# Half of wq of four heads on partitions 0 to 63: a decode step of attention and mixer on one core

## The chip, the core and the metric

The kernel runs on one core of a Trainium2 chip. Its engines are PE (matrix products; PEld is its loading of weights), DVE, ACT, POOL and SP. SP computes nothing here: it issues nearly every load, in order, and an instruction on SP that waits holds back all that stand behind it. The loads are carried by 16 DMA engines. The metric is the device time of one execution in microseconds (us).

## The reference

Two layers run over x of shape (2, 1, 512), each an attention block over a given cache and a token mixer, with a residual around each:

```
x = x + A(layernorm(x));  x = x + B(layernorm(x));  x = x + A(layernorm(x));  x = x + B(layernorm(x))
A: q = x @ wq (32 heads of 128);  p = softmax(q k^T / sqrt(128)) over 32768 keys;  (p v) @ wo
   8 key-value heads, 4 query heads on each; k and v are (2, 8, 32768, 128) in float32
B: u = gelu(layernorm(x)^T w1 + b1) with 1792 hidden units, then u w2 + b2, per channel
```

Both layers use the same weights and the same cache. All is float32.

## The kernel before

**Units.** A unit is (layer, batch, head): 2 x 2 x 8 = 32 of them. Each reads K and V of its batch and head once (16.8 MB each). A unit's K is 64 groups of 128 x 512, its V too; a step is four groups. `Order` lists all steps: the K steps of one unit, then the V steps of the unit before it, and so on. Only around the two places where a batch goes from layer 0 to layer 1 ("the changes") is the order another one, and some of K and V stays in SBUF and is used twice.

**Memory and loads.** The tile `mem` holds 106 cells of 128 partitions x 512 elements. A full load of K or V takes 32 cells (8.39 MB), so three of them and ten more cells fit. `plan_loads` decides while the program is built, from assumed times, which cells each load takes, how large it is and after which step it is issued; on the chip SP waits for semaphores until the cells are free. Around the changes the loads are small, and cells 90 to 105 go round among loads of four cells.

**Weights.** `wqo` holds for each head 4 cells of wq and 4 cells of wo. In nearly all of the program wq goes to cells 0 to 3, wo to cells 4 to 7. wq of a head is asked for 16 steps ahead of its first K step; wo of a head is in use until the `out_2` (L490) of its last unit.

**Queries.** `make_q` runs in three steps on PE and DVE. `wide_products` (L321) makes four products of a 128 x 32 column tile of `xw` (the normalized x, as columns) with 128 x 512 of wq, one for each quarter d of the 512 inputs, into four bands of 32 partitions of one PSUM tile; `narrow_products` (L328) adds the bands. The work sits among the V steps of the unit before, ten to six steps ahead of the K steps that need it.

**The rest.** K steps (L356) make scores, V steps (L424) make the weighted sums in `acc`, DVE and ACT do the softmax in between, `out_1` and `out_2` (L463, L490) multiply by wo. The last unit loads V in ever smaller pieces (16, 8, 4, 2, 1, 1 cells), and its mixer ends the program.

Of the kernel before, what the change touches and what calls it, by code (L numbers as in the profile page):

```python
# [8 lines left out]
F32 = mybir.dt.float32  # L9
# [4 lines left out]
P = 128  # L14
G = 512
# [5 lines left out]
WCELLS = 4  # L21
# [17 lines left out]
STEP_US = 1.6  # L39
ASK_Q = 16  # L40
ASK_O = 8


class Order:
# [75 lines left out]
def plan_loads(order, weights, busy):  # L120

    steps = order.steps
    step_of = {(kind, u, g + i): p for p, (kind, u, g) in enumerate(steps) for i in range(STEP)}
    from_kept = set(order.kept.values()) | set(order.held.values())
    asked = [(p, kind, u, g + i) for p, (kind, u, g) in enumerate(steps) for i in range(STEP)]
    asked = [a for a in asked if a[1:] not in from_kept]  # L130
    weights = sorted(weights)
    last_use = [-1] * CELLS
    landed, done, loads = {}, [], []
    queue, array, begun, i = 2.0, 0.0, -1, 0

    def ready(cells):
        t = 0.0
        for c in cells:
            if last_use[c] >= len(done):
                return None  # L140
            if last_use[c] >= 0:
                t = max(t, done[last_use[c]])
        return t

    while i < len(asked) or weights:
        if weights and (i == len(asked) or weights[0][0] <= asked[i][0]):
            _, name, last = weights.pop(0)
            label, sizes, stays = ("W", name, 0), (WCELLS,), True
        else:
            _, kind, u, g = asked[i]  # L150
            label, stays = (kind, u, g), (kind, u, g) in order.kept
            n = 1
            while (
                i + n < len(asked)
                and asked[i + n][1:] == (kind, u, g + n)
                and (g + n) % HALF
                and ((kind, u, g + n) in order.kept) == stays
            ):
                n += 1
            sizes = [s for s in SIZES if s <= n] or [n]  # L160
            if label in order.sizes:
                sizes = [min(order.sizes[label], n)]
        best = None
        for s in sizes:
            spots = range(CELLS - s + 1)
            found = None
            for a in spots if stays else reversed(spots):
                t = ready(range(a, a + s))
                if t is not None:
                    wait = max(0.0, t + LEAD_US - queue)  # L170
                    key = (wait, t if s == max(SIZES) or label[:2] == ("V", order.last) else 0.0)
                    if found is None or key < found[3]:
                        found = (wait, s, a, key)
            if found is not None and (best is None or found[0] < best[0] - 0.01):
                best = found
            if best is not None and best[0] == 0.0:
                break
        wait, s, a, _ = best
        begun = max(begun, *(last_use[a : a + s]))
        loads.append((label, s, a, begun))  # L180
        queue += wait + s * CELL_US + LOAD_US
        if label[0] == "W":
            last_use[a : a + s] = [last] * s
        else:
            for j in range(s):
                key = (kind, u, g + j)
                for k in (key, order.kept.get(key)):
                    if k is not None:
                        landed[k] = queue + LAND_US
                        last_use[a + j] = step_of[order.back.get(k, k)]  # L190
                if key in order.held:
                    landed[order.held[key]] = queue + LAND_US
            i += s
        while len(done) < len(steps):
            kind, u, g = steps[len(done)]
            keys = [(kind, u, g + j) for j in range(STEP)]
            if any(k not in landed for k in keys):
                break
            array = max(array, *(landed[k] for k in keys)) + STEP_US
            array += busy.get(len(done), 0.0)  # L200
            done.append(array)
    return loads


@with_exitstack
def gqa_mixer_kernel(ctx: ExitStack, tc: tile.TileContext, x, kt, v, wqo, cols, out):
    nc = tc.nc
    B, D = out.shape
    HKV = wqo.shape[0]
    R = wqo.shape[2] // (2 * D)  # L210
    DH = kt.shape[2]
    DT = D // P
# [7 lines left out]
    const = ctx.enter_context(tc.tile_pool(name="const", bufs=1))  # L220
# [10 lines left out]
    def cells(a, n):  # L231
        return mem[:, a * G : (a + n) * G]
# [18 lines left out]
    misc = pfix.tile([P, G], F32, name="misc")  # L251
    S = [const.tile([P, G], F32, name=f"S{k}") for k in range(2)]
    xw = const.tile([P, DT, 32], F32, name="xw")
    RAW = B
    xT = {}
    turn = [0, 0, 0]
# [7 lines left out]
    def constants():  # L264
# [4 lines left out]
        nc.gpsimd.memset(xw, 0.0)  # L269
        nc.gpsimd.memset(xw[:, :, RAW + 1], 1.0)  # L270
        nc.vector.tensor_reduce(
# [6 lines left out]
    def first_input():  # L278
# [16 lines left out]
        for b in range(B):  # L295
            xT[b] = xcols[:, b, :]
            nc.vector.tensor_scalar_mul(xw[:, :, b], cen[:, b, :], rs[:, b : b + 1])

    def row_tile():
        return work.tile([P, D], F32, name="row", bufs=1)  # L300

    wq_sb, wo_sb = {}, {}
    q_at, q_ps, q_row = {}, {}, {}
# [13 lines left out]
    def wide_products(us, wq):  # L317

        q_ps[us] = pfix.tile([P, G], F32, name="bcast")
        for d in range(DT):  # L320
            nc.tensor.matmul(q_ps[us][32 * d : 32 * d + 32, :], xw[:, d, :], wq[:, d, :], start=True, stop=True)  # L321

    def narrow_products(us, side):

# [289 lines left out]
    def change_0(key):  # L614
        xT[key[1]] = const.tile([P, DT], F32, name=f"xT_{key[1]}")
        nc.vector.tensor_add(xw[:, :, RAW], columns(key), sq)

# [141 lines left out]
    def at(p, f, *args, us=0.0):  # L759
        hooks.setdefault(p, []).append((f, args))  # L760
        busy[p] = busy.get(p, 0.0) + us
# [10 lines left out]
    for u in order.units:  # L772
        layer, b, h = u
# [5 lines left out]
        us = (u, mate) if b == 0 and mate not in made and (layer == 0 or h < HKV - 2) else (u,)  # L779
# [5 lines left out]
    for name, us in users.items():  # L785
        k0 = min(first["K", u] for u in us)
        h = name if isinstance(name, int) else name[1]
        layer = min(u[0] for u in us)
        v0 = min(first["V", u] for u in us)
        both = h >= HKV - 2  # L790
        weights.append((k0 - ASK_Q if k0 else -1, ("q", layer, h), max(first["K", u] for u in us) if both else k0))
        weights.append((k0 if both else v0 + ASK_O, ("o", layer, h), max(end["V", u, 1] for u in us) + 3))

    for u in order.units:
        layer, b, h = u
# [35 lines left out]
        e = v_end  # L831
# [23 lines left out]
        at(e + 3, unread, u, G)  # L855
        at(e + 4, change_3, y, us=1.0)
        at(e + 4, unread, u, G // 2)
        assert e + 4 < first["K", y]

    for x, _, y in order.changes:  # L860
# [10 lines left out]
    def load(label, n, a):  # L871
        kind, u, g = label
        if kind == "W":
            part, layer, h = u
            w = D * R
            at_w = 0 if part == "q" else w
            nc.sync.dma_start(cells(a, n), wqo[h][:, at_w : at_w + w])
            (wq_sb if part == "q" else wo_sb)[layer, h] = cells(a, n).rearrange("p (t c) -> p t c", t=DT)
            return
        layer, b, h = u  # L880
        src = (kt if kind == "K" else v)[b * HKV + h, g // HALF, :, (g % HALF) * G : (g % HALF + n) * G]
        nc.sync.dma_start(cells(a, n), src)
        for j in range(n):
            at_cell[kind, u, g + j] = a + j
            if (kind, u, g + j) in order.kept:
                at_cell[order.kept[kind, u, g + j]] = a + j
# [6 lines left out]
        load(label, n, a)  # L893
    constants()
    first_input()
    for step in range(3):
        make_q(opening_q, step)
    for p, (kind, u, g) in enumerate(steps):
# [8 lines left out]
def _layout(A_x, A_k_cache, A_v_cache, A_wq, A_wo, B_w1, B_b1, B_w2, B_b2):  # L907
    import numpy as np

    B, HKV, SK, DH = A_k_cache.shape  # L910
    D = A_x.shape[-1]
    U = B * HKV
    kt = A_k_cache.reshape(U, 2, NG, 32, 2, 2, 8, 2, 2, DH).transpose(0, 1, 9, 4, 7, 8, 2, 5, 6, 3)
    wq = A_wq.reshape(D // P, P, HKV, -1).transpose(2, 1, 0, 3)
    wo = A_wo.reshape(HKV, -1, DH, D).transpose(0, 2, 1, 3)
    w1, b1, w2 = (a.reshape(P, -1) for a in (B_w1, B_b1, B_w2))
    none = np.zeros_like(w2)
    w2z = np.stack([none, w2], axis=2).reshape(P, -1)
    cols = [w1, b1, w2z, none[:, :1], np.broadcast_to(B_b2.reshape(1, 1), (P, 1))]
    return {  # L920
        "x": np.ascontiguousarray(A_x.reshape(B * (D // P), P).T),
        "kt": np.ascontiguousarray(kt).reshape(U, 2, DH, HALF * G),
        "v": A_v_cache.reshape(U, 2, P, HALF * G),
        "wqo": np.concatenate([wq.reshape(HKV, P, -1), wo.reshape(HKV, DH, -1)], axis=2),
        "cols": np.concatenate(cols, axis=1),
    }


_INS = ["x", "kt", "v", "wqo", "cols"]


# [20 lines left out]
```

## Time and profile before

| | |
|---|---|
| median of 3 runs | 2503.35 us (2501.34 to 2504.8) |
| the profiled execution | 2500.76 us; its span, first to last instruction, 2498.1 us |
| busy | PE 56%, PEld 17%, DVE 8%, ACT 7% of the span |
| mean rate of the loads | 426 GB/s over the span, 1064.66 MB |
| matmul instructions of K steps, V steps | 4096, 4080 |

The page of the profile gives busy times by engine, the span in 40 slices, the DMA queues, the chain of work that ended last, and groups of instructions. The table by windows gives, for stretches of time, each engine's busy time, then the granted clock of TensorE, then the mean share of the 16 DMA engines that were busy, then the rate in GB/s. In short windows a transfer is counted where it falls, so a share can go a little above 1. A logical float32 product shows as two instructions on PE. In the timeline each row is a start, a duration, an engine, a line, what is written from what, a count, and in brackets how long the engine stood idle before it and for what.

### The profile page before, as it was taken

How to read it: one execution, taken by the hardware profiler on the slowest of the kernel's cores; microseconds unless marked ns; L12 is line 12 of the kernel's file. 1: busy time of each engine (PE TensorE's matmuls, PEld its weight loads, DVE VectorE, ACT ScalarE, POOL GpSimd, SP SyncE). 2: the span in 40 equal slices, each digit the busy share in tenths (PEclk: the TensorE clock that was granted, in tenths of full speed). 3: DMA queues.
4: the chain of work that ended last, by engine and by line, in shares of the span. 5: the costliest groups of instructions: out<-in, count | busy, mean ns of one | idle time of the engine just before them, and what ended most of it. 6: DMA issues, size and time to landing. Idle time of an engine off the chain costs nothing.

```text
span 2498.1 us, 21381 instructions
## 1 busy us (share of the span) xinstructions
PE 1393.4 (56%) x9754; PEld 412.7 (17%) x9754; DVE 188.6 (8%) x502; ACT 186.9 (7%) x581; POOL 5.1 (0%) x18
## 2 busy tenths in 40 slices
PE   3455455555555545556776775555555545564557
PEld 1111111111111111112121221111111111111113
DVE  1000000000000000001111010000000000000012
ACT  0100000000000000001110210000000000000021
POOL 0000000000000000000000000000000000000000
PEclk8777777777777777778887986777777777776788
DMA  9999999999999999999999999999999999999996
GB/s 420 435 435 431 431 435 429 435 426 434 436 431 435 433 425 436 425 435 406 417 430 423 418 427 437 431 434 434 428 434 431 436 432 429 435 435 433 432 428 272
DMA packets 34947, 1064.66 MB, mean 426 GB/s; under 512 B 4133, under 2 KB 4137, under 8 KB 5034
## 3 DMA queue, kind: packets, MB, share of 16 engines
q1 hardware_dynamic: 34568, 1063.27, 99.1%
q8 instruction: 76, 1.25, 0.2%
q14 instruction: 13, 0.11, 0.0%
q10 hardware_dynamic: 290, 0.04, 0.0%
HBM read 1063.29 MB, written 0.00 MB: 426 GB/s over the span
## 4 chain that ended last, share of the span: by engine, by line
DMA 64%; PE 25%; another core or an unknown queue 9%; issue 0%; DVE 0%; ACT 0%; SPq 0%; POOLq 0%; DVEq 0%
DMA mem<-in_v_dram 35%; DMA mem<-in_kt_dram 29%; PE acc L424 13%; PE scores L356 8%; PE misc L463 1%; PE rows L490 0%; PE misc L328 0%; PE bcast L321 0%; PE misc L447 0%; PE misc L380 0%; PE rows L724 0%; ACT S L406 0%; PE misc L374 0%; PE bcast L516 0%
## 5 line engine op out<-in xcount | busy, mean ns | idle before, releaser
L424 PE MATMUL acc<-mem,S 128*16 128x512 f32 x4080 | 594.7, 717 | 585.3 <-DMA mem<-in_v_dram 580.5
L356 PE MATMUL scores<-mem,qz 128*32 128x512 f32 x4096 | 613.6, 741 | 487.4 <-DMA mem<-in_kt_dram 487.2
L406 ACT ACTIVATE S<-S,neg 128x128 f32<-128x128 f32 x256 | 129.6, 509 | 2215.9 <-DVE S L401 1202.8
L356 PEld LDWEIGHTS scores<-mem,qz 128*32 128x32 f32 x4096 | 145.3, 129 | 887.9 <-issue 795.5
L424 PEld LDWEIGHTS acc<-mem,S 128*16 128x16 f32 x4080 | 127.5, 107 | 900.6 <-issue 808.6
L366 DVE TENSOR_REDUCE mx<-scores 128x1 f32<-128x512 f32 x64 | 44.3, 692 | 775.0 <-PE scores L356 767.2
L463 PEld LDWEIGHTS misc<-selg,row 128*128 128x128 f32 x256 | 48.9, 285 | 48.2 <-issue 36.8
L401 DVE STREAM_TRANSPOSE S<-scores 128x512 f32<-128x512 f32 x64 | 45.5, 710 | 126.4 <-PE acc L424 126.4
L463 PE MATMUL misc<-selg,row 128*128 128x4 f32 x256 | 51.7, 325 | 3.3 <-DVE row L455 3.3
L490 PE MATMUL rows<-mem,oz 128*2 128x512 f32 x248 | 51.2, 914 | 0.3 <-DVE oz L479 0.3
L406 ACT ACTIVATION_READ_ACCUMULATOR S<-S,neg 128x1 f32 x256 | 47.7, 187 | 0.0
L376 DVE TENSOR_REDUCE m<-misc 1x4 f32<-1x128 f32 x32 | 8.9, 279 | 379.5 <-PE misc L374 379.5
L455 DVE COPY row<-acc 128x512 f32<-128x512 f32 x32 | 22.1, 692 | 177.9 <-PE acc L424 177.9
L449 DVE RECIPROCAL rl<-misc 128x4 f32<-128x4 f32 x32 | 5.8, 183 | 352.8 <-PE misc L447 352.8
L479 DVE TENSOR_TENSOR oz<-misc,rl 128x4 f32<-128x4 f32 x32 | 5.2, 163 | 276.6 <-PE misc L463 276.2
L447 PEld LDWEIGHTS misc<-both,one 128*128 128x128 f32 x64 | 12.8, 250 | 51.5 <-issue 44.4
L321 PE MATMUL bcast<-mem,xw 128*32 128x512 f32 x144 | 20.0, 618 | 1.7 <-POOL x_rs L294 1.7
L328 PEld LDWEIGHTS misc<-selg,row 128*128 128x128 f32 x128 | 17.1, 208 | 18.7 <-issue 7.7
L328 PE MATMUL misc<-selg,row 128*128 128x2 f32 (+1 forms) x128 | 18.5, 266 | 0.8 <-DVE row L313 0.8
L574 ACT ACTIVATE row<-bcast,bias,scale 128x512 f32<-128x512 f32 x21 | 16.3, 778 | 31.6 <-PE rows L558 15.4
L447 PE MATMUL misc<-both,one 128*128 128x4 f32 x64 | 15.6, 315 | 5.2 <-DVE both L446 5.2
L374 PE MATMUL misc<-ident,mxa 128*1 128x128 f32 x64 | 17.1, 363 | 2.0 <-DVE mxa L372 2.0
(125 smaller groups left out, 263.4 us busy)
## 6 DMA issues: line engine op xcount, KB each, us to landing
mem<-in_v_dram SPq DMA_DIRECT2D x13, 4096.0 KB, 25.1
mem<-in_v_dram SPq DMA_DIRECT2D x37, 1024.0 KB, 9.0
mem<-in_kt_dram SPq DMA_DIRECT2D x15, 2048.0 KB, 17.6
mem<-in_kt_dram SPq DMA_DIRECT2D x30, 1024.0 KB, 9.1
mem<-in_wqo_dram SPq DMA_DIRECT2D x28, 1024.0 KB, 36.3
mem<-in_kt_dram SPq DMA_DIRECT2D x6, 4096.0 KB, 28.6
mem<-in_kt_dram SPq DMA_DIRECT2D x2, 6144.0 KB, 23.5
mem<-in_v_dram SPq DMA_DIRECT2D x3, 2048.0 KB, 38.2
```

Source lines behind the costliest of these rows:

```text
L321: nc.tensor.matmul(q_ps[us][32 * d : 32 * d + 32, :], xw[:, d, :], wq[:, d, :], start=True, stop=True)
L328: nc.tensor.matmul(pt[:, r * n : (r + 1) * n], q_row[us][:, r * DH : (r + 1) * DH], side, start=True, stop=True,)
L356: nc.tensor.matmul(sc_ps[u, half][32 * row : 32 * row + 32, :], qz[:, at : at + 32], cells(at_cell["K", u, g], 1), start=(i == 0), stop=(i ...
L366: nc.vector.tensor_reduce(mx[u][:, half : half + 1], sc_ps[u, half], axis=AX.X, op=ALU.max)
L374: nc.tensor.matmul(pm[:1, :P], mxa, ident, start=True, stop=True)
L401: nc.vector.transpose(S[half], sc_ps[u, half])
L406: nc.scalar.activation(s[:, :, h], s[:, :, h], AF.Exp, bias=neg[u][:, h : h + 1], scale=SCALE, accum_out=lsum[u][:, half, h : h + 1],)
L424: nc.tensor.matmul(acc[32 * row : 32 * row + R * QT, :], S[half][:, col : col + R * QT], vc, start=(g < NG), stop=(g >= quads - NG),)
L447: nc.tensor.matmul(pl[:, :R], ones, both, start=True, stop=True)
L455: nc.vector.tensor_copy(asb[u], acc)
L463: nc.tensor.matmul(po_of[u][:, :R], asb[u][:, t * DH : (t + 1) * DH], selg[:, t * R : (t + 1) * R], start=(t == 0), stop=(t == QT - 1 and ...
L490: nc.tensor.matmul(rows[32 * r : 32 * r + B, :], oT[u][:, 2 * r + 1 - b : 2 * r + 3 - b], wo_of(u)[:, r, :], start=False, stop=(u == order ...
```

## The change

For four heads (layer 0: 2 and 4; layer 1: 3 and 1) wq takes 6 cells instead of 4. The first two quarters of wq (d = 0, 1) are loaded as before, 128 partitions with half as long a row. The other two quarters (d = 2, 3) lie on partitions 0 to 63 alone, over four cells: of each quarter rows 0 to 63 in one cell and rows 64 to 127 in the next. They come from a new input `low`, by two transfers of 32 partitions each. In `low` every four rows are followed by a fifth that isn't read, so that the source has eight groups of four rows. The bytes that are read are the same, 1 MiB for each head.

The products of d = 2 and d = 3 become two each, over 64 rows: one with rows 0 to 63 of `xw`, one with `high`, a copy of rows 64 to 127 of `xw` on partitions 0 to 63. DVE makes `high` three times (`lift`): once at the start and once in each change. The scratch that is set aside for descriptors of POOL's queue becomes 256 instead of 512.

```diff
+LOWER = (("q", 0, 2), ("q", 0, 4), ("q", 1, 3), ("q", 1, 1))
+LOWER_CELLS = 6
...
-            label, sizes, stays = ("W", name, 0), (WCELLS,), True
+            label, sizes, stays = ("W", name, 0), (LOWER_CELLS if name in LOWER else WCELLS,), True
...
+    high = const.tile([P // 2, DT // 2, 32], F32, name="high")
...
+    def lift():
+
+        nc.vector.tensor_copy(high, xw[P // 2 :, DT // 2 :, :])
...
         for d in range(DT):
-            nc.tensor.matmul(q_ps[us][32 * d : 32 * d + 32, :], xw[:, d, :], wq[:, d, :], start=True, stop=True)
+            to = q_ps[us][32 * d : 32 * d + 32, :]
+            if d < DT // 2 or wq.shape[1] == DT:
+                nc.tensor.matmul(to, xw[:, d, :], wq[:, d, :], start=True, stop=True)
+                continue
+            half, k = P // 2, d - DT // 2
+            nc.tensor.matmul(to, xw[:half, d, :], wq[:half, DT // 2 + 2 * k, :], start=True, stop=False)
+            nc.tensor.matmul(to, high[:, k, :], wq[:half, DT // 2 + 2 * k + 1, :], start=False, stop=True)
...
+            if u in LOWER:
+                nc.sync.dma_start(cells(a, DT // 2), wqo[h][:, : w // 2])
+                for k in range(2):
+                    to = cells(a + DT // 2, DT)[32 * k : 32 * k + 32, :]
+                    nc.sync.dma_start(to, low[h, k][:, :4, :])
+                wq_sb[layer, h] = cells(a, n).rearrange("p (t c) -> p t c", t=n)
+                return
...
+    low = np.zeros((HKV, 2, 8, 5, 4 * G), np.float32)
+    part = wq[:, :, D // P // 2:, :].reshape(HKV, 2, 2, 8, 4, -1, G).transpose(0, 2, 3, 4, 5, 1, 6)
+    low[:, :, :, :4, :] = part.reshape(HKV, 2, 8, 4, 4 * G)
...
-    nc = bacc.Bacc("TRN2", target_bir_lowering=False, num_devices=1, dynamic_dma_scratch_size=512)
+    nc = bacc.Bacc("TRN2", target_bir_lowering=False, num_devices=1, dynamic_dma_scratch_size=256)
```

All K and V loads keep their sizes, their cells and their places in the order. For the four heads wq stands in cells 0 to 5 and wo in cells 6 to 9.

On SP, where the weights of head 2 are loaded in layer 0 (the first of the four places; `in_wqo_dram` holds the weights, PE_49 is a semaphore that PE raises), before:

```order
L882 DMA mem<-in_kt_dram 128x16384 [waits DMAHW5_49,PE_49]
L877 DMA mem<-in_wqo_dram 128x2048 [waits DMAHW1_49]
L882 DMA mem<-in_v_dram 128x16384 [waits DMAHW6_49,PE_49]
L877 DMA mem<-in_wqo_dram 128x2048 [waits PE_49]
L882 DMA mem<-in_v_dram 128x16384 [waits DMAHW7_49,PE_49]
```

The same place after:

```order
L903 DMA mem<-in_kt_dram 128x16384 [waits DMAHW5_49,PE_49]
L892 DMA mem<-in_wqo_dram 128x1024 [waits DMAHW1_49]
L895 DMA mem<-in_low_dram 32x1x2048 [waits PE_49]
L895 DMA mem<-in_low_dram 32x1x2048
L903 DMA mem<-in_v_dram 128x16384 [waits DMAHW6_49]
L898 DMA mem<-in_wqo_dram 128x2048 [waits PE_49]
L903 DMA mem<-in_v_dram 128x16384 [waits DMAHW7_49,PE_49]
```

The wait for PE that stood ahead of the load of wo (until L490 has read the wo of the head before, cells 4 and 5 of it) now stands ahead of the first `low` load as well, and so ahead of a V load that it did not hold before.

On PE, where the queries of head 2 in layer 0 are made, before:

```order
L424 MATMUL acc<-mem,S_89 16x512 x12
L321 MATMUL bcast<-mem,xw 32x512 x4
L424 MATMUL acc<-mem,S_89 16x512 x4
L424 MATMUL acc<-mem,S_90 16x512 x8
L447 MATMUL misc<-both,one 128x4
```

After:

```order
L437 MATMUL acc<-mem,S_89 16x512 x12
L330 MATMUL bcast<-mem,xw 32x512 x2
L333 MATMUL bcast<-mem,xw 32x512
L334 MATMUL bcast<-mem,high 32x512
L333 MATMUL bcast<-mem,xw 32x512
L334 MATMUL bcast<-mem,high 32x512
L437 MATMUL acc<-mem,S_89 16x512 x4
L437 MATMUL acc<-mem,S_90 16x512 x8
L460 MATMUL misc<-both,one 128x4
```

Two more products stand there, among the V steps of the unit before; nothing else moved.

More of the change, by code (lines that the diff above doesn't have):

```diff
@@ L205, in gqa_mixer_kernel @@
 @with_exitstack
-def gqa_mixer_kernel(ctx: ExitStack, tc: tile.TileContext, x, kt, v, wqo, cols, out):
+def gqa_mixer_kernel(ctx: ExitStack, tc: tile.TileContext, x, kt, v, wqo, low, cols, out):
     nc = tc.nc
@@ L857, in gqa_mixer_kernel @@
         at(e + 4, unread, u, G // 2)
+        at(e + 7, lift)
         assert e + 4 < first["K", y]
@@ L895, in gqa_mixer_kernel @@
     first_input()
+    lift()
     for step in range(3):
@@ L924, in _layout @@
         "wqo": np.concatenate([wq.reshape(HKV, P, -1), wo.reshape(HKV, DH, -1)], axis=2),
+        "low": low,
         "cols": np.concatenate(cols, axis=1),
     }
-_INS = ["x", "kt", "v", "wqo", "cols"]
+_INS = ["x", "kt", "v", "wqo", "low", "cols"]
 def kernel(A_x, A_k_cache, A_v_cache, A_wq, A_wo, B_x, B_w1, B_b1, B_w2, B_b2):
```

## The prediction

> **What bounds the kernel now.** I read the page first: busy times, DMA queues, the chain.
>
> ```profile
> span 2498.1 us, 21381 instructions
> ...
> PE 1393.4 (56%) x9754; PEld 412.7 (17%) x9754; DVE 188.6 (8%) x502; ACT 186.9 (7%) x581; POOL 5.1 (0%) x18
> ...
> q1 hardware_dynamic: 34568, 1063.27, 99.1%
> q8 instruction: 76, 1.25, 0.2%
> ...
> DMA 64%; PE 25%; another core or an unknown queue 9%; issue 0%; DVE 0%; ACT 0%; SPq 0%; POOLq 0%; DVEq 0%
> ```
>
> The loads' queue (q1) takes 99.1% of what 16 DMA engines have in the span. The engines are full, PE is not. Since the bytes stay the same, time can only come from engines that are full while others are not. So I looked for moments when the share falls, in the table by windows (the last two columns are DMA share and GB/s). First the steady state:
>
> ```profile
> 256.00:580.00 324.00, 168.77 (x1144) 48.87 (x1144) 19.26 (x50) 16.88 (x64) 0.00 (x0) 0.73 1.00 433
> ```
>
> Then the end of the last loads:
>
> ```profile
> 2471.00:2472.00 1.00, 1.00 (x12) 0.26 (x8) 0.00 (x0) 0.00 (x0) 0.00 (x0) 1.00 0.97 395
> 2472.00:2473.00 1.00, 1.00 (x16) 0.36 (x12) 0.00 (x0) 0.00 (x0) 0.00 (x0) 1.00 0.87 348
> 2473.00:2474.00 1.00, 1.00 (x15) 0.30 (x7) 0.00 (x0) 0.00 (x0) 0.00 (x0) 1.00 0.59 244
> 2474.00:2475.00 1.00, 0.36 (x4) 0.06 (x1) 0.00 (x0) 0.00 (x0) 0.00 (x0) 1.00 0.53 221
> 2475.00:2476.00 1.00, 0.88 (x10) 0.26 (x14) 0.00 (x0) 0.00 (x0) 0.00 (x0) 1.00 0.47 197
> 2476.00:2477.00 1.00, 1.00 (x14) 0.32 (x7) 0.00 (x0) 0.00 (x0) 0.00 (x0) 1.00 0.49 199
> 2477.00:2478.00 1.00, 1.00 (x27) 0.83 (x25) 0.69 (x1) 0.00 (x0) 0.00 (x0) 1.00 0.54 203
> 2478.00:2479.00 1.00, 1.00 (x28) 0.73 (x20) 0.00 (x0) 0.00 (x0) 0.00 (x0) 1.00 0.35 133
> 2479.00:2480.00 1.00, 1.00 (x20) 0.98 (x22) 0.00 (x0) 0.00 (x0) 0.00 (x0) 1.00 0.04 14
> ```
>
> The share doesn't fall to nothing. It falls to one half and stays there from 2473.5 to 2478.5: eight engines are done, eight have 5 us of work left. Every load is shared over all 16, so it has landed only when the late eight are done. Where the 5 us come from, the page's q8 row says: 76 fetches of instructions take 0.2% of 16 x 2498.1 us, that is 80 us (60 to 100 with the rounding). Spread over 16 engines this would be 5 us each and no difference. On eight of them it is 10 us each, about 5 in each half of the run.
>
> The same in the middle, at the first change:
>
> ```profile
> 1160.00:1175.00 15.00, 11.44 (x74) 3.27 (x74) 1.03 (x4) 2.11 (x8) 0.00 (x0) 0.77 0.99 415
> 1175.00:1180.00 5.00, 4.67 (x34) 1.83 (x34) 2.42 (x5) 2.66 (x9) 0.00 (x0) 1.00 0.82 313
> 1180.00:1185.00 5.00, 3.52 (x32) 1.98 (x35) 1.79 (x7) 2.05 (x4) 0.54 (x1) 1.00 1.05 382
> 1185.00:1190.00 5.00, 4.20 (x43) 1.33 (x39) 0.00 (x0) 3.27 (x5) 0.00 (x0) 1.00 0.98 392
> 1190.00:1195.00 5.00, 3.02 (x36) 0.83 (x32) 0.00 (x0) 2.89 (x4) 0.00 (x0) 1.00 1.00 388
> 1195.00:1205.00 10.00, 6.14 (x63) 2.41 (x56) 1.77 (x5) 4.38 (x6) 0.00 (x0) 1.00 1.02 425
> ```
>
> Between 1175 and 1195 some 1125 GB/s x us are missing against 425, which is 2.65 us of all engines or 5.3 us of eight. Here the loads go round among a few cells, so the early eight must wait for cells that PE frees only after the late eight have delivered. There they lose their lead, and in the second half of the run it grows again. So the late eight set the pace in both halves.
>
> **The change part by part.** *Bytes off the late eight.* At 433 GB/s one engine moves 27.06 GB/s. A wq load of 1 MiB is 64 KiB or 2.42 us on each. After the change the first half costs every engine 32 KiB, 1.21 us, and the `low` transfers, with eight groups of source rows, can fall on eight engines alone: 64 KiB or 2.42 us on each of these. So at each of four places eight engines save 1.21 us and eight pay 1.21 us more. Two places lie in each half of the run, so a lead of about 5 us shrinks by 4.84 to nearly nothing. If the late eight are the ones relieved, they finish 2.42 us earlier at the first change and 2.42 us earlier again at the end: -4.84 us. The paying eight stay at or ahead of them by then, so they cost nothing.
>
> Which eight? No row names the engine of a packet. But one other transfer leaves engines out:
>
> ```profile
> out_dram<-row ACTq DMA_DIRECT2D x1, 2.0 KB
> ```
>
> It is one row, so one engine carries it, and the records of single packets around it show that this engine ended its shares with the early eight. If a transfer of fewer groups starts from the same engine, `low` falls on the early eight. [...]
>
> *Less starving at the first change.* The 2.65 us missing there exceed the 2.42 that a lead of 4.84 on eight engines explains, and against the 433 of the steady state they would be more, some 3.2. What is left, 0 to 0.8 us, all engines lose while loads arrive apart. I take 0.4.
>
> *Shorter rows.* The first half has rows of 4 KB instead of 8, and there are eight more loads. No window holds such loads alone. From the long rows of the steady state (433 GB/s) to the 8 KB rows of the small loads (425, from 1195 to 1205) it is 2%; as much again for 4 KB is 0.02 us a place. I take +0.1 for all, between 0 and 0.3.
>
> *The wait on SP.* The order shows that the first `low` load waits for L490, and the V load behind it waits too.
>
> ```profile
> 197.93 0.42 SPq L877 DMA_DIRECT2D mem<-in_wqo_dram  x1
> 215.57 0.33 SPq L882 DMA_DIRECT2D mem<-in_v_dram  x1
> 231.13 1.93 PE L490 MATMUL rows<-mem,oz 128*2 128x512 f32 x8
> 233.12 0.33 SPq L877 DMA_DIRECT2D mem<-in_wqo_dram  x1
> 238.61 0.33 SPq L882 DMA_DIRECT2D mem<-in_v_dram  x1
> 266.95 3.62 PE L424 MATMUL acc<-mem,S 128*16 128x512 f32 x16 [12.03 <-DMA mem<-in_v_dram]
> 275.65 1.04 PE L321 MATMUL bcast<-mem,xw 128*32 128x512 f32 x8
> ```
>
> The V load goes out at about 233.5 instead of 215.57, 18 us later. PE got its data at 266.9. Its 8.39 MB take 19.4 us at 433 GB/s, so its first bytes moved at about 247.5. Issued at 233.5 it is still 14 us early, and so are the `low` loads ahead of it, which land near 250 and are read at 275.65. wo and the next V load (238.61) keep their times. Cost nothing, at the price of 18 of 32 us of cover.
>
> *Products and copies.* Two more logical products at four places are 16 instructions. The page's row for L321 prices them:
>
> ```profile
> L321 PE MATMUL bcast<-mem,xw 128*32 128x512 f32 x144 | 20.0, 618 | 1.7 <-POOL x_rs L294 1.7
> ```
>
> By 139 ns of busy time each (20.0/144) that is 0.6 us a place, by their own 618 ns 2.5 us. At 266.95 PE had idled 12.03 us for data, so either is hidden. A `lift` copies 64 x 64; DVE rows of the start price it:
>
> ```profile
> 9.97 0.36 DVE L297 TENSOR_SCALAR xw<-cen,x_rs 128x4 f32<-128x4 f32 x2 [0.83 <-POOL x_rs L294]
> 12.43 0.69 DVE L313 COPY row<-bcast 128x512 f32<-128x512 f32 x1 [2.10 <-PE bcast L321]
> 15.08 0.23 DVE L342 COPY qz<-misc 128x4 f32<-128x4 f32 x2 [1.96 <-PE misc L328]
> 25.83 8.52 PE L356 MATMUL scores<-mem,qz 128*32 128x512 f32 x64 [10.79 <-DMA mem<-in_kt_dram]
> ```
>
> It lies between 0.12 and 0.69 us, and the start has 10 us until data come. In the changes it stands between copying `acc` and the product by wo, where loads are late, not DVE.
>
> Sum: -4.84 - 0.4 + 0.1 = -5.1 us. The profiled execution (2500.76 us, 2498.1 of it span) would take 2495.7; the median of the runs shown, 2503.35, is 2.6 above it, so I forecast 2498.2. What a measurement here can tell from no change is about 0.2%, 5.0 us, which puts the border at 2498.3, almost on the forecast.
>
> **Rivals.** *The wrong eight.* If `low` falls on the late eight, these pay 4.84 us and the early ones wait longer: +4.84 and up to 0.8 more starving, 2508.2 to 2509.0. Against it stands the one-row transfer; for it, that no row names an engine.
>
> *Half-width transfers hold the others up* (the one on the slower side that I take most seriously). If all engines wait until `low` is done, each place costs 1.21 us more for everyone: +4.84, 2508.2, and with a gap of a microsecond behind each of eight transfers 2516. It decides as soon as the idle eight can't take up the next load. Against it: in the windows from 2473.5 to 2478.5 one half works on alone at half the rate, having been left behind by engines that went ahead through many loads. [...]
>
> *The queue runs dry.* If the wait for L490 ended 14 us later, the V load would be late at four places, a microsecond for each beyond that.
>
> *Half of it.* If what is won at the first change is lost there again (PE's chain, not the late eight, sets when cells come free), only the end's 2.42 stays: 2500.9.
>
> *The change doesn't do what it says.* If `low` is spread over all engines after all, nothing is moved: 2503.4.
>
> **How the numbers follow.** Forecast 0.76 (2496 to 2500, the border inside it, two thirds of it below since what starves at the change may give more); wrong eight 0.05; holding up 0.04; dry queue 0.02; half 0.08; no shift 0.05. Faster by over 0.2%: 0.52. Within: 0.24 of the forecast, half and no shift, 0.37. Slower: 0.11. The range 2496.0 to 2503.5 leaves out the slower cases and a little at the fast end.
>
> **What would show it.** In the changed profile the half share at the end should last 1 us or less instead of 5, and the rate from 1175 to 1195 should be near 420. SP should issue the V load at the four places near its wo load. The share in the steady windows should stay at 1.00 around 245 to 250. A half share at the end of 10 us would mean the wrong eight; a dip near 250 the holding up or the dry queue.

## The result, and the profile after

The changed kernel takes 2506.02 us (median of 15 runs, 2503.91 to 2510.49), the kernel before, measured together with it, 2500.57 us (15 runs, 2498.95 to 2504.8). The ratio is 1.0021 [1.0013, 1.0029]: 5.45 us slower, where 5.1 us faster was forecast. Two places show where it goes: the end of the last loads and the first change. First the page of the changed kernel:

```profile
span 2504.7 us, 21425 instructions
...
q1 hardware_dynamic: 34888, 1063.27, 98.9%
q8 instruction: 77, 1.26, 0.2%
```

The same bytes, the same full queue, one more fetch of instructions. Next the windows at the end of the loads and at the first change (columns as before: busy time by engine, clock, DMA share, GB/s):

```profile
2479.00:2480.00 1.00, 1.00 (x16) 0.24 (x12) 0.00 (x0) 0.00 (x0) 0.00 (x0) 1.00 0.88 358
2480.00:2481.00 1.00, 1.00 (x14) 0.30 (x7) 0.00 (x0) 0.00 (x0) 0.00 (x0) 1.00 0.85 332
2481.00:2482.00 1.00, 0.45 (x8) 0.13 (x2) 0.00 (x0) 0.00 (x0) 0.00 (x0) 1.00 0.49 193
2482.00:2483.00 1.00, 0.81 (x8) 0.25 (x12) 0.00 (x0) 0.00 (x0) 0.00 (x0) 1.00 0.33 117
2483.00:2484.00 1.00, 1.00 (x13) 0.28 (x6) 0.00 (x0) 0.00 (x0) 0.00 (x0) 1.00 0.16 66
2484.00:2485.00 1.00, 1.00 (x26) 0.82 (x22) 0.69 (x1) 0.00 (x0) 0.00 (x0) 1.00 0.13 53
2485.00:2486.00 1.00, 1.00 (x31) 0.72 (x20) 0.00 (x0) 0.00 (x0) 0.00 (x0) 1.00 0.13 49
2486.00:2487.00 1.00, 1.00 (x20) 0.98 (x23) 0.00 (x0) 0.00 (x0) 0.00 (x0) 1.00 0.07 29
```

```profile
1160.00:1175.00 15.00, 10.82 (x82) 3.09 (x74) 0.95 (x3) 2.11 (x8) 0.00 (x0) 0.88 1.00 421
1175.00:1180.00 5.00, 3.82 (x36) 1.44 (x32) 1.48 (x3) 0.57 (x3) 0.00 (x0) 1.00 0.90 374
1180.00:1185.00 5.00, 3.51 (x26) 0.81 (x22) 2.92 (x8) 3.09 (x9) 0.55 (x1) 1.00 0.88 333
1185.00:1190.00 5.00, 4.41 (x48) 2.34 (x40) 0.22 (x1) 2.19 (x4) 0.00 (x0) 1.00 0.93 339
1190.00:1195.00 5.00, 3.40 (x40) 0.90 (x34) 0.00 (x0) 3.60 (x6) 0.00 (x0) 1.00 0.95 329
1195.00:1205.00 10.00, 5.37 (x64) 1.36 (x54) 0.85 (x2) 5.83 (x9) 0.00 (x0) 1.00 0.99 392
```

The half share is gone, and in its place is a staircase. To 2481 some 14 engines work, and from 2483 to 2486 the share is 0.13 to 0.16: **two engines of 16** are still at it. At the first change 1625 GB/s x us are missing against 425 between 1175 and 1195 (20 x 425 less 5 x (374 + 333 + 339 + 329)) where 1125 were missing before. One profile doesn't settle that, though: the kernel called "The wait without the placement" below, whose median is that of the kernel before, misses 1540 in these windows of its own profile (342, 375, 336 and 339 GB/s).

The trace also holds the times at which a load's semaphore was raised, once by each engine that has delivered its share ("landings" below). A full load has 16 of them; a `low` transfer has eight, behind one record at its issue, so eight engines carry it. The landings don't name the engine, but they come in an order that hardly changes from one full load to the next: across each of the first 25 fetches of instructions in the profile before, 15 of the 16 landings keep their distances within 0.1 us, and one moves. So one engine can be followed. Here is one K load of the first half, shortly before the first change, in ns after its first landing:

```
before, at 881.75 us: 0 146 310 587 922 1382 1400 1458 | 4593 4613 4623 4687 4753 4805 4987 5473
after,  at 879.58 us: 0 51 | 4345 4421 4431 4512 4532 4618 4810 5006 5140 5969 5979 5997 | 9841 10294
```

Before: eight early, eight late, as the prediction read it. After: 2, 12 and 2. A place (one of the four loads of wq in the new way) puts 1.21 us more on each engine that carries `low` and takes 1.21 us from each other one (an estimate: 32 KiB at 27.06 GB/s, a sixteenth of the 433 of the steady state), so the two kinds move 2.42 us apart, and two places lie ahead of this load: 4.84 us. If two of the late eight are among the engines that carry `low`, then two early ones stay early, six early ones rise by 4.84 to where the late ones were, six late ones stay, and two late ones rise from about 5 to between 9.8 and 10.3, all counted from the first landing. These are the groups that the list shows.

That two of the eight are late ones can be seen without this sum, in the landings of `low` itself. Here is the first `low` transfer of each of the first two places, again in ns after its first landing:

```
first place,  at 245.19 us: 0 290 357 398 527 579 1251 2468
second place, at 566.03 us: 0 259 327 495 530 1219 1921 3935
```

Six of the eight keep their distances within 50 ns. Two don't: 398 becomes 1921, and 2468 becomes 3935, each 1.5 us later. Between the two places instructions were fetched at 299.6 and at 333.0 us, the eighth and the ninth fetch, and in the full loads behind each of the two one of these engines falls back.

What the two cost is seen in the last landing of a load. Of the K load above it comes 2.64 us later than before; in all nine full loads from 744 to 882 us it is 2.62 to 2.68. At the end of the last load the groups are the same:

```
before, at 2473.03 us: 0 96 136 239 665 888 1064 1176 | 5162 5931 6128 6142 6216 6311 6411 7045
after,  at 2476.04 us: 0 748 | 4734 4750 4865 5750 5795 6260 6380 6426 6568 7594 7642 7755 | 11022 11070
```

There the last landing comes 7.04 us later. Not all of that is from the places: between 1062 and 1261 us of the kernel before, over the first change, the delay of the last landing grew from 2.63 to 4.49 us, and in the kernel called "The wait without the placement" it grew as much (from 0.17 to 2.08).

The wait on SP and the added products are where they were expected: `low` goes out when `out_2` (now L503) ends at 233.20, and V right behind it (timelines of SP, then of PE, at the first place):

```profile
197.02 0.42 SPq L892 DMA_DIRECT2D mem<-in_wqo_dram  x1
233.23 1.55 SPq L895 DMA_DIRECT2D mem<-in_low_dram  x2
234.83 0.44 SPq L903 DMA_DIRECT2D mem<-in_v_dram  x1
235.31 0.43 SPq L898 DMA_DIRECT2D mem<-in_wqo_dram  x1
```

```profile
231.27 1.93 PE L503 MATMUL rows<-mem,oz 128*2 128x512 f32 x8
...
268.42 3.62 PE L437 MATMUL acc<-mem,S 128*16 128x512 f32 x16 [14.40 <-DMA mem<-in_v_dram]
...
278.06 1.05 PE L333 MATMUL bcast<-mem,xw 64*32 64x512 f32 x4
278.94 1.03 PE L334 MATMUL bcast<-mem,high 64*32 64x512 f32 x4
```

### The profile page after: what moved, and what is told of

Same layout as the page of the kernel before. It is cut to its first block, busy times and chain, and to the rows that moved or that the text cites. A ratio compares the mean times of both kernels' runs of the same rounds, so it can differ in the third digit from the quotient of the medians.

```text
span 2504.7 us, 21425 instructions
## 1 busy us (share of the span) xinstructions
PE 1401.2 (56%) x9770; PEld 415.4 (17%) x9770; DVE 189.3 (8%) x505; ACT 187.0 (7%) x581; POOL 5.2 (0%) x18
## 4 chain that ended last, share of the span: by engine, by line
DMA 62%; PE 27%; another core or an unknown queue 10%; DVE 1%; issue 0%; ACT 0%; SPq 0%; POOLq 0%; DVEq 0%
DMA mem<-in_v_dram 34%; DMA mem<-in_kt_dram 28%; PE acc L437 12%; PE scores L369 10%; PE misc L476 1%; PE rows L503 1%; PE misc L341 1%; PE bcast L330 0%; PE misc L460 0%; PE misc L393 0%; PE misc L668 0%; ACT S L419 0%; SPq L895 0%; PE misc L387 0%
## 5 line engine op out<-in xcount | busy, mean ns | idle before, releaser
L369 PE MATMUL scores<-mem,qz 128*32 128x512 f32 x4096 | 605.8, 733 | 487.7 <-DMA mem<-in_kt_dram 487.6
L503 PE MATMUL rows<-mem,oz 128*2 128x512 f32 x248 | 51.9, 925 | 0.3 <-DVE oz L492 0.3
```

The source lines that it names most:

```text
L369: nc.tensor.matmul(sc_ps[u, half][32 * row : 32 * row + 32, :], qz[:, at : at + 32], cells(at_cell["K", u, g], 1), start=(i == 0), stop=(i ...
L503: nc.tensor.matmul(rows[32 * r : 32 * r + B, :], oT[u][:, 2 * r + 1 - b : 2 * r + 3 - b], wo_of(u)[:, r, :], start=False, stop=(u == order ...
```

## Experiments

Theory A, in the form that the landings above gave it: `low` falls on eight engines, two of which also fetch instructions; these two set the time. Theory B: the wait, the six cells, the copies or the rows cost the time. Each ratio below is against the kernel before, with its 95% interval.

**`low` over all 16 engines.** The padding is left out, so that a transfer's source is 32 rows in one piece.

```diff
-                    nc.sync.dma_start(to, low[h, k][:, :4, :])
+                    nc.sync.dma_start(to, low[h, k])
```

> The changed kernel with the padding left out of the new input: cells, the wait on SP, half-depth products and copies stay, but the 32 source rows of each transfer are contiguous, so that all 16 engines can share it. Theory A (two of the eight engines that carry the half-wide loads are also among the eight that fetch instructions; they pay at every place and set the pace): the loss goes, about 2500.6 us, within 1.5 us of the kernel before. Theory B (the wait that now stands ahead of a V load, the products or the cells cost the time): it stays at about 2506. Theory C (64 partitions alone are written at half the rate, whichever engines write them): it stays at 2505 or more.

Measured: 2518.91 us, ratio 1.0068 [1.0054, 1.0081]. By its words this falls to theory C ("2505 or more"), but C's half rate would cost 4 x 1.21 = 4.84 us, and 17.4 were lost. The windows from 242 to 250 of this kernel, then of the changed one:

```profile
242.00:246.00 4.00, 0.26 (x4) 0.23 (x8) 0.00 (x0) 0.00 (x0) 0.00 (x0) 0.67 1.04 261
246.00:250.00 4.00, 4.00 (x21) 0.91 (x17) 0.00 (x0) 0.00 (x0) 0.00 (x0) 0.50 1.05 263
```

```profile
242.00:246.00 4.00, 0.72 (x4) 0.23 (x8) 0.00 (x0) 0.00 (x0) 0.00 (x0) 0.50 0.96 399
246.00:250.00 4.00, 4.00 (x32) 1.15 (x28) 0.00 (x0) 0.00 (x0) 0.00 (x0) 0.66 1.20 518
```

All engines are busy (a share of 1.04 and 1.05), at 60% of the rate (261 and 263 of 433 GB/s). Across the first place the mean landing of a load, that is the mean of its 16 landings, falls back by 3.2 us, where the changed kernel's moves by 0.04. So it wasn't a clean test of A: with 16 engines on these 64 partitions all fall behind, by 3.2 us, and with eight, on four rows each, the mean stays where it was. Nor is C the cause of the change's own loss: a half rate that held up all engines would move its mean by 1.21 us a place.

**Two places instead of four.**

```diff
-LOWER = (("q", 0, 2), ("q", 0, 4), ("q", 1, 3), ("q", 1, 1))
+LOWER = (("q", 0, 2), ("q", 1, 3))
```

> The changed kernel with heads 2 (layer 0) and 3 (layer 1) alone loaded in the new way, one place in each half of the run instead of two. Theory A: the slowest engine pays 1.21 us a place, so half of the loss goes: about 2503. Theory B and C, a fixed price by place: also about 2503. A loss that comes only where the late engines are overtaken twice: under 2501.5.

Measured: 2502.45 us, ratio 1.0006 [0.9997, 1.0015]. Half of 1.0021 lies in the interval, none too. It fits a loss that grows with the places, and tells no more.

**The wait without the placement.** Six cells, wait and copies stay, but the second half of wq is loaded over all 128 partitions, and the products are of full depth.

```diff
-                for k in range(2):
-                    to = cells(a + DT // 2, DT)[32 * k : 32 * k + 32, :]
-                    nc.sync.dma_start(to, low[h, k][:, :4, :])
+                nc.sync.dma_start(cells(a + DT, DT // 2), wqo[h][:, w // 2 : w])
```

> The changed kernel with the second half of wq loaded over all 128 partitions again, into cells 4 and 5 of the six, with full-depth products. What stays of the change: six cells, the second load of wq behind the wait for L490 and ahead of the V load, shorter rows, the copies. What goes: loads that fall on eight engines alone. Theory A (the two engines that both fetch instructions and carry the half-wide loads): 2500.5 to 2502 us, as before within 0.06%. Theory B (the wait or the cells): 2505 to 2507.

Measured: 2501.4 us, ratio 1.0000 [0.9991, 1.0009]. Theory B falls. The products of half depth are gone here as well, but in the changed kernel they stand behind 14.40 us in which PE waits for data. What costs time is where the bytes of `low` go.

**Which engines? Two probes.** `low` is cut into transfers of other numbers of groups, to see by the landings which engines take part. The engines are counted by an assumption of the author's, which no run shows: that a transfer of k groups falls on the same k first engines each time. In the first probe, mostly groups of 8 to 16 rows; in the second, groups of four rows (at the first place 6, 2 and 8 groups).

```diff
+    ("q", 0, 2): ((4, 8), (2, 16)),
+    ("q", 0, 4): ((6, 8), (16, 1)),
...
+    ("q", 0, 2): ((6, 4), (2, 4), (8, 4)),
+    ("q", 0, 4): ((5, 4), (3, 4), (8, 4)),
```

> The changed kernel with the 64 rows of each place cut in other ways: 4 groups of 8 and 2 of 16 in the first place, 6 of 8 (the rest over 16) in the second, 7 of 9 and a single row in the third, 5 of 12 (and 4 single rows) in the fourth. It is to show which of the first eight engines also fetch instructions, from the landings of each part against those of the load ahead of it. Theory A: two of the eight are late ones. If the half-wide loads fall on the first engines in number, the parts of 4 and 2 groups show whether the two are among the first four. The time says little: engines with 4 groups pay 2.4 to 7.2 us more, so 2505 to 2515.

> The changed kernel with the first 32 of the 64 rows of each place cut into groups of four in other ways: 6 and 2 groups, 5 and 3, 7 and 1, 4 and 4; the other 32 rows stay 8 groups. It is to show which two of the first eight engines fetch instructions. From the probe before, engines 0 to 3 did not fall behind by fetches from 268 to 546 us, so theory A has the two among 4 to 7: the 6-group part holds none, one or both of them. Time 2504 to 2512.

Measured, one run each: 2521.64 us and 2506.35 us. In the first, groups of 8 and 16 rows take longer than their bytes do in full loads (two groups of 16 rows begin to land 8.6 us after four of 8 rows began, where 128 KiB take 4.84 us at 27.06 GB/s), and most landings can't be told apart. One thing can: the four engines that four groups fall on stay at 3.3, 3.8, 7.3 and 9.5 us after the first landing from 268 to 546 us, while eight others jump, one after another, by 1.2 to 1.55 us: a fetch for each. So the first four engines, by this count, fetch nothing in this stretch, in which each of the eight jumps once. In the second probe the six groups of the first place land by engines of which none had been hit by a fetch of 16 KB so far, the one hit first (2.34 us late) not among them. From this I took it that the first six fetch nothing, and that the two are the seventh and eighth. That was too much: the eighth engine in the rotation had not had its turn yet.

**Six groups, eight groups.** Only the last quarter of wq is moved, at six heads. In the one kernel it lies in six groups over three cells (and small copies build a 56-row form of x), in the other in eight groups over two cells.

```diff
-                nc.sync.dma_start(cells(a, DT // 2), wqo[h][:, : w // 2])
+                nc.sync.dma_start(cells(a, DT - 1), wqo[h][:, : w - G])
...
-    low = np.zeros((HKV, 2, 8, 5, 4 * G), np.float32)
+    low = np.zeros((HKV, 2, 6, 5, 3, G), np.float32)
```

> Only the last quarter of wq (256 KiB, with unused space 288 KiB) goes to the lower partitions, in six source groups instead of eight, at six heads instead of four (three in each half of the run). With six groups the transfers fall on six DMA engines, which in the two probes hold none of those that fetch instructions. Theory A (two of the first eight engines also fetch, and they set the time): here all engines that fetch are relieved of 16 KiB, 0.605 us by 27.06 GB/s, at each of six places, 3.6 us in all, and the six that pay 1.2 us more at a place stay within the 4 to 5 us by which they lead in each half. So about 2497.5, ratio 0.9986, faster. Rival D (any transfer to part of the partitions costs time whichever engines carry it, about 1.2 us a place): slower, ratio 1.002 to 1.003. Rival E (the lead is lost again at the first change, only the end counts): ratio 0.9993. The rest of the quarter needs small transfers to build the 56-row copy of x in each change; if these cost, up to 2 us for each change come on top.

> The same quarter at the same six heads, but in eight groups, as in the change: the two engines that fetch and lie among the first eight carry 32 KiB of the quarter in place of 16, 0.605 us more at each of six places. Theory A: 3.6 us slower, ratio 1.0014, while the kernel with six groups is 3.6 us faster: 7 us between two kernels that load the same quarter and differ in which engines carry it. Rival D (the cost does not depend on which engines): both on the same side, within 0.1% of each other. That the unused space at the end of rows or the small copies decide: the two differ by less than 2 us.

Measured: six groups 2508.68 us, ratio 1.0037 [1.0023, 1.0051]; eight groups 2504.89 us, ratio 1.0015 [1.0006, 1.0024]. Eight groups cost what A said (1.0014). Six groups were to gain and lost 7.2 us. Their landings say why. The first of the two six-group transfers, ns after its first landing:

```
first place,  245.55 us: 0 128 591 659 763 1428
second place, 406.72 us: 0 556 643 711 1369 1633
```

Five of the six keep their distances within 60 ns. One has gone from 128 to 1633: it was hit between the two, by the eighth fetch, at 300 us. So one of the two that fetch is among the first six; as none is among the first four, it is the fifth or sixth. It pays 1.21 us at six places, 7.3 us, and 7.2 were measured. The size fits, but this was worked out after the run, and so close a fit is partly luck, as the end of this section shows.

**Four groups.** The last quarter at the change's four heads, on four engines: four rows each on partitions 0 to 15, 32 to 47, 64 to 79 and 96 to 111.

```diff
-                for k in range(2):
-                    to = cells(a + DT // 2, DT)[32 * k : 32 * k + 32, :]
+                for k in range(4):
+                    to = cells(a + DT - 1, 2)[32 * k : 32 * k + 16, :]
```

> The last quarter of wq (256 KiB) at the four heads of the change, in four transfers of four source groups each, so on four DMA engines: 64 KiB on each of these where 16 KiB lay, 1.8 us more at a place, and 0.605 us less on the twelve others. Theory A as the landings of the six-group run leave it (of the eight engines that fetch, one is the fifth or sixth, one the seventh or eighth, none among the first four): all engines that fetch are relieved, and the four that pay keep behind them (3.6 us in each half against a lead of 4 to 5), so 4 x 0.605 = 2.4 us faster, ratio 0.9990, and the four-group landings at each place belong to engines that no fetch has delayed. If one of the first four fetches after all: 4 x 1.81 = 7.3 us slower, ratio 1.0029. Rival D (transfers to part of the partitions cost about 1.2 us a place whichever engines carry them): ratio 1.002 or more.

Measured: 2504.71 us, ratio 1.0016 [1.0007, 1.0025]. No gain either, though the four keep their distances within 0.3 us from the first place to the second, less than a fetch costs (1.2 to 1.55 us in the first probe). The transfers to the two lower bands took 0.63 and 0.65 us, those to the two upper ones 1.40 and 1.27, and at the first place the mean landing of all 16 fell back by 1.5 us against the kernel before. Either four small transfers cost this, or partitions 64 to 127 do. The next two kernels part these.

**Four groups on lower partitions alone; eight groups on upper ones.** The first keeps to partitions 0 to 15 and 32 to 47: rows 0 to 63 of the last quarter, at eight heads. Rows 64 to 127 are loaded over all 128 partitions, with half the columns on each. The second is the changed kernel with `low` on partitions 64 to 127.

```diff
+                nc.sync.dma_start(cells(a, DT)[:, : w - G // 2], wqh[h])
+                for k in range(2):
+                    to = cells(a + DT, 2)[32 * k : 32 * k + 16, :]
...
-                    to = cells(a + DT // 2, DT)[32 * k : 32 * k + 32, :]
+                    to = cells(a + DT // 2, DT)[64 + 32 * k : 96 + 32 * k, :]
```

> As the run with four groups, but on partitions 0 to 15 and 32 to 47 alone: rows 0 to 63 of the last quarter (128 KiB) go there in two transfers of four groups; rows 64 to 127 of it are loaded over all 128 partitions with half of the columns on each. Eight heads, four in each half of the run. Each of the first four DMA engines carries 24 KiB more at a place (0.9 us), the twelve others 8 KiB less (0.3 us). Theory A (only which engines carry the bytes counts, on partitions that they share with none): 8 x 0.30 = 2.4 us faster, ratio 0.9990, and the mean landing of all 16 engines does not jump at the places, as it did by 1.5 us with four groups on all bands. Theory A without a gain at the first change: ratio 0.9995. If the four-group run lost its 4 us to the groups themselves (four engines, four small transfers) and not to partitions 64 to 127: the mean jumps here too, by some 0.4 us and more a place, ratio 1.001 or above.

> The changed kernel with its two transfers of eight groups onto partitions 64 to 127 instead of 0 to 63 (the operands are swapped to suit), everything else as in the change. It tests why the run with four groups lost: there the two transfers onto partitions 64 to 111 took 1.3 us where those onto 0 to 47 took 0.63, and all 16 engines lay 1.5 us later after each place. If the first eight engines share partitions 64 to 127 with the other eight: each transfer takes 2.5 us or more instead of 1.24, the mean of all engines jumps by 3 us or more at each place, 12 us and more in all, ratio 1.005 to 1.010. If the partitions do not matter: like the change, ratio 1.002.

Measured: on upper partitions 2524.15 us, ratio 1.0087 [1.0072, 1.0103]; four groups on lower partitions 2500.11 us, ratio 0.9997 [0.9988, 1.0006]. On the upper partitions a transfer takes 2.47 us where it took 1.24, and the mean landing falls back by 3.5 us at the first place. Its windows:

```profile
242.00:246.00 4.00, 0.00 (x0) 0.00 (x0) 0.00 (x0) 0.00 (x0) 0.00 (x0) 0.53 0.95 248
246.00:250.00 4.00, 3.84 (x24) 1.17 (x28) 0.00 (x0) 0.00 (x0) 0.00 (x0) 0.62 1.28 317
```

Again busy engines (a share of 0.95 and 1.28) at a low rate (248 and 317 GB/s), as with 16 engines on 64 partitions. Four groups on the lower partitions don't show that: each transfer takes 0.63 us, the mean landing moves by 0.04 us, and at the four places of the first half the landings keep the same distances (0, 200, 690, 1410 ns within 25), so no fetch falls on any of the four there. But the gain of 2.4 us did not come out. In the profiled execution the mean landing drifted by 0.6 us from 243 to 1062 us, over the four places of the first half, and the last landing gained 0.1 us instead of 1.2; why is not shown. The interval holds 0.9990 and 1.0000 alike. No kernel here is measurably faster than the one before.

The shift of the landings across the first place, against the kernel before (us; the K load at 242.7, then the V load at 264.5), and the whole runs beside A's sums:

```
                             first   mean   last  | A, four to eight places  measured
the change, eight groups     -1.07  +0.04  +1.30  | 4 x 1.21  = +4.8           +5.45
wait without the placement   +0.05  +0.06  +0.06  | 0                          +0.4
last quarter, eight groups   -0.37  +0.04  +0.19  | 6 x 0.605 = +3.6           +3.4
last quarter, six groups     -0.51  +0.13  +0.24  | 6 x 1.21  = +7.3 (after)   +7.2
four groups, lower           -0.27  +0.04  +0.19  | -8 x 0.30 = -2.4           -0.1
four groups, all bands       +0.84  +1.51  +2.58  | -2.4, without the bands    +4.3
16 engines on 64 partitions  +3.27  +3.19  +2.66  | none                      +17.4
eight groups, upper          +2.37  +3.53  +4.93  | none                      +24.0
```

The first five rows move no mean by more than 0.13 us: time is only carried from some engines to others. The last three lose time on all. "Last" shows the first place only; where the engine that pays is not yet the slowest there, it becomes so later (six groups: +0.24 here, +3.57 in the K load of the next table).

A's sums take the engine that pays for the latest one all along. The K load at 881.75 us tests them without what the changes add. Its last landing comes later than in the kernel before by:

```
                            A       this load   full loads from 744 to 904 us
the change                  +2.42   +2.64       +2.62 to +4.21
two places                  +1.21   +1.02       -0.52 to +1.03
last quarter, six groups    +3.63   +3.57       +1.98 to +3.60
last quarter, eight groups  +1.82   +2.05       +0.49 to +2.06
wait without the placement  0       +0.21       +0.20 to +0.22
```

In this load A comes out within 0.25 us. In its neighbours the difference depends on which engine has fetched last (the 25th fetch is at 899.1 us in the change, at 913.4 before), and A can be 1.8 us off. So the sums hold while a payer is the latest, and the agreement of whole runs with them to a few tenths is in part luck.

## Why the prediction was wrong

- **Which eight?** This is the step that failed. It took "the eight that are late" and "the eight that `low` uses" for two groups that are either the same or apart, because one transfer of one row ended with the early ones, and it let `low` start at that row's engine, which no run shows. That row shows one engine, and that engine is indeed early: the packet of the V load behind the row ended at 2414.33 or 2414.34 us, and that load's early landings run from 2414.61 to 2415.78, the late ones from 2419.48 on. The landings show that the groups overlap in two engines. The prediction's words "the paying eight stay at or ahead of them by then, so they cost nothing" are true of six and false of two. What sets a load's end is its slowest engine, so two that pay weigh as much as eight: ahead of the first change the last landing came 2.64 us later, where 2.42 us earlier was forecast.
- **Bytes off the late eight.** The price was right: 1.21 us forecast, 1.24 us between the mean landings of the two `low` transfers; and in the K load before the first change the two last landings stand 4.85 and 4.82 us farther behind the first one than the two last did before, where 4.84 are to be expected. Six of the late eight are relieved as it said. It helps nothing, because the other two carry 2.42 us more in each of the two halves.
- **Less starving at the first change.** No gain of 0.4 us is seen: some 3.8 us are missing (1625/425) where 2.65 were before. But 3.6 us (1540/425) are missing in the profile of the kernel that has the wait without the placement, so whether the placement changes this term stays open.
- **Shorter rows, the wait on SP, products and copies.** Right, to what can be measured: the kernel that keeps wait, cells, copies and the shorter rows stands at 1.0000. The V load goes out at 234.83, forecast 233.5. The products of half depth take 1.05 and 1.03 us for four, behind an idle time of 14.40 us.
- **The rivals.** *The wrong eight* gave the right time (+4.84 to +5.6) by a case that the trace excludes: the share at the end falls to two engines (0.13 to 0.16), not to a half. *Half-width transfers hold the others up* is wrong for eight engines on partitions 0 to 63 (the mean moves by 0.04 us; the share from 256 to 580 is 1.00), and right for 16 engines on these partitions and for eight on 64 to 127: 3.2 and 3.5 us at the first place. A transfer takes 2.47 us on the upper partitions against 1.24 on the lower ones; why the two differ is not shown.

The steady state is the same as before:

```profile
256.00:580.00 324.00, 171.17 (x1148) 49.11 (x1148) 19.27 (x50) 16.88 (x64) 0.00 (x0) 0.74 1.00 432
```

Left open: whether the engines are rightly counted, which of the fifth and sixth, and of the seventh and eighth engine, is then the one that fetches, and whether the four engines that are free of it can be used for a gain that a measurement shows. Open too is how the 5.45 us divide: the sum of the places is 4.84, but the delay that the profiled execution gathers over the first change (1.9 us in the last landing) is as large in that of the wait without the placement (1.9 us), at equal medians. So of one profile only the drift between the changes can be used.

## What to carry to other kernels

When bytes are moved from some DMA engines to others, a group's mean tells nothing (here it moved by 0.04 us at the first place, and the kernel took 5.45 us more): find out for every engine on the receiving side how late it already is, since one late engine among them undoes the whole (in the kernel with six groups it was one of six, and 7.2 us were lost). A trace that names no engines still tells this by the order of a load's landings, followed through time. And read the rate beside the DMA share: where 16 engines wrote 64 partitions, the share was 1.04 and 1.05 at 60% of the rate of the steady state.

## What was not expected of the hardware

- Fetches of instructions (77 of 16 KB in the changed kernel) go round eight engines, two of them among the eight that carry `low` and six among the others. Before, the fetches 1, 9, 17 and 25 put back the same landing, from 0.76 to 2.29, 3.84, 5.43 and 7.01 us behind the first, and seven others move in between, one for each fetch. Each of the first 25 delays its engine by 1.41 to 1.56 us (one goes from 0.23 to 1.69 between the loads at 286 and 306 us), and nothing makes up for it until the loads wait for cells: the last landing is 7.0 us behind the first at 1088 us, and 2.9 at 1196.
- 512 KiB by eight engines with four rows each on partitions 0 to 63 hold nobody up (the mean landing moves by 0.04 us). The same on partitions 64 to 127 take twice the time (2.47 us a transfer against 1.24), and by 16 engines on 64 partitions all engines lie 3.2 us later.
